# Output copy ahead of the gate's products, and the first two attentions laid out anew, in an attention and expert kernel

## The chip, the cores and the metric

The kernel runs on one core of one Trainium2 chip. The metric is the device time of one execution in microseconds (us). The engines are TensorE (PE), VectorE (DVE), ScalarE (ACT), GpSimd (POOL) and SyncE (SP). DMAs are issued from SP's, ScalarE's and GpSimd's queues.

## The reference

Attention over 8 batches with 16 query heads on 4 key heads, 384 positions and a head size of 64, and behind it a two-level gate that sends each position to one of 16 experts. An expert is two matrices with a relu between them.

```python
q (8, 16, 384, 64)   k, v (8, 4, 384, 64)
k, v = np.repeat(k, 4, axis=1), np.repeat(v, 4, axis=1)
attn = softmax(q @ k.transpose(0, 1, 3, 2) / 8)
x = (attn @ v).transpose(0, 2, 1, 3).reshape(3072, 1024)

g_idx = argmax(x @ w_group);  g_w = its softmax weight        # 4 groups
e_idx = argmax(x @ w_expert[g]);  e_w = its softmax weight    # 4 experts in each
h = np.maximum(x @ w1[g, e], 0.0)                             # 1024 x 1024
out = (g_w * e_w)[:, None] * (h @ w2[g, e])                   # 1024 x 1024
```

## The kernel before, in words

The work goes batch by batch, and every engine's order is written out by hand: the scheduler is off for the whole body. Behind the body a loop handles positions whose expert was not the one fetched for their batch; it runs no times here.

**One attention** (class `Attn`) has 24 units: four key heads, six blocks of 64 keys each. At step `u`, `run` scores unit `u + 2` on TensorE (`score`, which also issues the exponential on ScalarE into a tile `e`), multiplies unit `u` with the values (`pv`), and calls `tail`. At every second unit `tail` adds two exponential tiles on GpSimd (`pair`), unless the unit is in `apart`. `lags` tells at which step VectorE reduces which pair to row sums (`reduce`; a unit in `apart` gives two reductions in place of an addition and one). After six units the products are copied out of PSUM to `xT`, on ScalarE for the heads in `act_copies`, on VectorE for the others. The `steps` dictionaries add further work behind given steps.

**Sums and division.** `join_keys` adds the partial sums on VectorE, `sums` spreads them over the partitions by a small matmul and takes the reciprocal, `normalise(b, m)` makes a tile `rb` of the factors (a transpose) and multiplies `xT` by it, and `cast(b, m)` makes the bf16 copy `xb` that the expert's first matmuls (`moe_h`) read. There are four `m` to a batch.

**PSUM.** `ps_tile` deals out two buffers for scores and expert products ("s") and two for products, sums and gate ("o"); "x" takes the "o" buffer that is not the current one.

**A block.** While one batch's attention has ended, `block(b)` does the expert of batch `f = b - 1`: `moe_h`, then three chunks of `ffn_y`, with the sums, divisions and gate of batch `b` between them, and the first two scores of batch `b + 1`. `y_out(f, c, y)` is the output copy: ScalarE multiplies chunk `c` of the expert's products by the gate's weight on the way from PSUM to `ot`, and two DMAs on SP's queue write it out (with `late`, VectorE does it).

**Loads.** Weights (fetched as soon as the expert number is known, by `pick_w1` and `pick_w2`), keys and queries come by DMAs from GpSimd's queue with a cast to bf16; keys and queries are then transposed by DMAs on SP's queue (`before_attention`). The weights of batch `b` are used in the block after the one that fetches them. Values come by SP's queue, and `sum_v` adds them up on GpSimd for a guess of the expert.

Of the kernel before, what the change touches and what calls it, by code (L numbers as in the profile page):

```python
# [9 lines left out]
F32 = mybir.dt.float32  # L10
# [8 lines left out]
def kernel(  # L19
# [11 lines left out]
    nc = tc.nc  # L31
# [24 lines left out]
    qpool = ctx.enter_context(tc.tile_pool(name="qload", bufs=2))  # L56
    vpool = ctx.enter_context(tc.tile_pool(name="v", bufs=2))
    epool = ctx.enter_context(tc.tile_pool(name="exp", bufs=13))
# [41 lines left out]
    def load_q(b, src=None):  # L100
        qraw[b] = qpool.tile([P, KQ, NC * D], BF16, name="q_raw")
        nc.gpsimd.dma_start(out=qraw[b], in_=rows(q[b] if src is None else src))
# [311 lines left out]
    def normalise(b, m, which=None):  # L414
        if b not in xb:
            xb[b] = xpool.tile([P, KQ, S], BF16, name="xb")
        ks = slice(2 * m, 2 * m + 2)
        rb = ps_tile(which)[:, :, :S] if which else gpool.tile([P, 2, S], F32, name="rb")
        nc.vector.transpose(  # L419
            out=rb.rearrange("p k (j x) -> p k j x", x=32),  # L420
            in_=inv[b][:, ks].unsqueeze(3).to_broadcast([P, 2, NB, 32]))
        x = xT[b][:, ks, :]
        nc.vector.tensor_mul(out=x, in0=x, in1=rb)  # L423

    def cast(b, m):
        ks = slice(2 * m, 2 * m + 2)
        nc.scalar.copy(out=xb[b][:, ks, :], in_=xT[b][:, ks, :])  # L427
# [205 lines left out]
    def before_attention(b):  # L633

        if b + 1 < B:
# [8 lines left out]
    at = {0: Attn(0, apart=(1, 3, 7, 9, 17, 23), act_copies=(0, 1, 3), lags={3: [1, 3], 7: [5, 7], 9: [9], 12: [11], 16: [13], 18: [15], 21: [17], 23: [19]}),  # L644
          1: Attn(1, apart=(3, 5), act_copies=(3,), lags={5: [1], 8: [3], 10: [5], 12: [7, 9], 13: [11], 15: [13], 18: [15], 20: [17], 22: [19], 23: [21]})}
# [21 lines left out]
    def x_logits(b):  # L667
# [13 lines left out]
        17: [do(pick_w1, 0), do(join_keys, 0, 0, 2), do(pick_w2, 0)],  # L681
        22: [do(sums, 0, 0, 2, "x")],
        23: [do(at[0].reduce, NU - 3)],
# [8 lines left out]
    def first_softmax():  # L692
# [6 lines left out]

    steps1 = {  # L700
        1: [
            do(at[0].reduce, NU - 1),
            do(normalise, 0, 0),
            do(cast, 0, 0),
            do(normalise, 0, 1, "x"),
        ],
        3: [do(join_keys, 0, 2, Hkv), do(sums, 0, 2, Hkv, "x"), do(cast, 0, 1)],
        6: [do(normalise, 0, 2, "x"), do(normalise, 0, 3, "x")],
        8: [do(load_k, 2)],
        9: [do(cast, 0, 2), do(load_q, 2)],  # L710
        10: [do(cast, 0, 3)],
        14: [do(moe_h, 0, 0, "s"), x_gate_logits],
        15: [
# [9 lines left out]
        18: [do(join_keys, 1, 0, 2), do(before_attention, 1)],  # L723
# [5 lines left out]
    def first_block():  # L729
        load_v(3)  # L730
        moe_y(0, 0, "s")
        load_k(3)
        load_q(3)
        sum_v(2)
        at[1].reduce(NU - 1)
        join_keys(1, 2, Hkv)
        normalise(1, 1)
        cast(1, 0)
        cast(1, 1)
        moe_y(0, 1, "s")  # L740
        sums(1, 2, Hkv, "o")
        normalise(1, 2)
        normalise(1, 3)
        cast(1, 2)
        y = ffn_y(w2s[0], hTs[0], 2, "o", (0,))
        at[2] = Attn(2)
        at[2].score(0)
        ffn_y(w2s[0], hTs[0], 2, "o", (1,), y)
        at[2].score(1)
        return do(y_out, 0, 2, y, True)  # L750
# [16 lines left out]
    def block(b):  # L767
# [4 lines left out]
        if b + 2 < B:  # L772
            load_k(b + 2)
            load_q(b + 2)
        pick_w1(b)
        pick_w2(b)
        if not last:
            sum_v(b + 1)
        moe_h(f, 0, "s")
# [21 lines left out]
        cast(b, 3)  # L801
        gate_logits(b, pt)
# [4 lines left out]
        y_out(f, 1, y)  # L807
        if not last:
            at[b + 1].score(1)
# [148 lines left out]
```

## Time and profile before

| | |
|---|---|
| median of 3 runs | 395.7 us (395.08 to 395.71) |
| profiled execution | 394.66 us |
| its span in the profile | 393.0 us |
| busy: TensorE, VectorE, ScalarE, GpSimd | 93%, 65%, 58%, 52% |
| TensorE's mean granted clock | 0.973 of full speed |

The span runs from the first to the last instruction of the profiled execution; 1.66 us of its time lie outside. Busy shares are means over stages that have different limits. The granted clock is a share of TensorE's full 2.4 GHz; in any moment it is at 1.0 (2.4 GHz) or at 0.5 (1.2 GHz), and a figure between is a mean over a stretch.

### The profile page before, as it was taken

How to read it: one execution, taken by the hardware profiler on the slowest of the kernel's cores; microseconds unless marked ns; L12 is line 12 of the kernel's file. 1: busy time of each engine (PE TensorE's matmuls, PEld its weight loads, DVE VectorE, ACT ScalarE, POOL GpSimd, SP SyncE). 2: the span in 40 equal slices, each digit the busy share in tenths (PEclk: the TensorE clock that was granted, in tenths of full speed). 3: DMA queues.
4: the chain of work that ended last, by engine and by line, in shares of the span. 5: the costliest groups of instructions: out<-in, count | busy, mean ns of one | idle time of the engine just before them, and what ended most of it. 6: DMA issues, size and time to landing. Idle time of an engine off the chain costs nothing.

```text
span 393.0 us, 9216 instructions
## 1 busy us (share of the span) xinstructions
PE 365.5 (93%) x3815; PEld 186.7 (48%) x3815; DVE 255.4 (65%) x470; ACT 226.2 (58%) x298; POOL 203.5 (52%) x156
## 2 busy tenths in 40 slices
PE   7996999999999899989999899998999989999993
PEld 3442455445554345544555445543455445464541
DVE  3989775886787576844778446784567756684121
ACT  4895755478634496444944459343792539634330
POOL 8175481946980199503993059920698009930000
PEclk9999899999999899998999989998999999999997
DMA  8969995999989993999929999399993993079924
GB/s 198 192 108 207 213 194 80 185 253 211 180 157 203 251 212 105 131 236 235 201 56 167 229 233 185 66 177 224 215 177 51 211 237 96 3 126 201 261 55 111
DMA packets 69325, 67.14 MB, mean 171 GB/s; under 512 B 37112, under 2 KB 49400, under 8 KB 69280
## 3 DMA queue, kind: packets, MB, share of 16 engines
q0 software_dynamic: 26640, 41.03, 60.5%
q1 hardware_dynamic: 42288, 25.01, 29.4%
q8 instruction: 32, 0.52, 0.5%
q10 hardware_dynamic: 352, 0.48, 0.5%
q14 instruction: 13, 0.11, 0.1%
HBM read 86.07 MB, written 12.58 MB: 251 GB/s over the span
## 4 chain that ended last, share of the span: by engine, by line
PE 71%; DVE 15%; ACT 6%; issue 3%; POOL 3%; DMA 1%; SPq 0%; POOLq 0%; DVEq 0%; ACTq 0%
PE ps_o L327 27%; PE ps_s L588 11%; PE ps_s L602 10%; PE ps_o L602 8%; PE ps_s L308 8%; DVE xT L423 4%; DVE rb L419 4%; PE ps_o L435 3%; DVE inv L412 3%; POOL e L335 3%; DVE red L344 2%; ACT e L314 2%; ACT xb L427 2%; ACT ot L621 1%; PE ps_o L588 1%
## 5 line engine op out<-in xcount | busy, mean ns | idle before, releaser
L335 POOL TENSOR_TENSOR e<-e 128x768 f32<-128x768 f32 x88 | 157.3, 1823 | 128.3 <-PE ps_s L308 114.9
L314 ACT ACTIVATE e<-ps_s 128x768 f32<-128x768 f32 x192 | 151.7, 813 | 49.9 <-PE ps_s L308 47.8
L327 PE MATMUL ps_o<-e,v_raw 64*64 64x384 f32 x1536 | 155.0, 487 | 0.4 <-DVE oh_all L539 0.4
L344 DVE TRANSPOSE_TENSOR_REDUCE red<-e 128x24 f32<-128x768 f32 x104 | 99.6, 971 | 43.3 <-POOL e L335 42.8
L588 PE MATMUL ps_s<-xb,w 128*128 128x384 bf16 x480 | 80.8, 326 | 0.0
L308 PE MATMUL ps_s<-qT,kT 64*64 64x384 bf16 x768 | 65.6, 329 | 11.6 <-ACT ot L621 9.6
L327 PEld LDWEIGHTS ps_o<-e,v_raw 64*64 64x64 f32 x1536 | 56.2, 134 | 38.9 <-issue 30.4
L588 PEld LDWEIGHTS <-w 128*128 128x128 bf16 x512 | 49.4, 98 | 36.0 <-issue 4.8
L602 PEld LDWEIGHTS <-hT 128*128 128x128 bf16 x384 | 37.7, 102 | 54.5 <-issue 12.9
L602 PE MATMUL ps_s<-w,hT 128*128 128x512 bf16 x248 | 57.3, 379 | 2.2 <-ACT hT L595 1.4
L308 PEld LDWEIGHTS <-kT 64*64 64x64 bf16 x768 | 24.6, 106 | 48.9 <-issue 45.8
L592 ACT ACTIVATE hT<-ps_s 128x768 bf16<-128x768 f32 x23 | 18.6, 810 | 43.4 <-PE ps_s L588 39.1
L427 ACT CAST xb<-xT 128x768 bf16<-128x768 f32 x28 | 23.2, 830 | 29.1 <-DVE xT L423 29.1
L602 PE MATMUL ps_o<-w,hT 128*128 128x512 bf16 x136 | 37.9, 439 | 0.0
L419 DVE STREAM_TRANSPOSE rb<-inv 128x768 f32<-128x768 f32 x28 | 27.3, 977 | 0.9
L423 DVE TENSOR_TENSOR xT<-xT,rb 128x768 f32<-128x768 f32 x27 | 26.7, 989 | 1.0
L369 DVE COPY xT<-ps_o 128x768 f32<-128x768 f32 x27 | 24.9, 922 | 1.3 <-PE ps_o L327 1.3
L621 ACT ACTIVATE ot<-ps_s,we 128x1024 f32<-128x1024 f32 x14 | 15.6, 1114 | 10.0 <-PE ps_s L602 9.2
L456 DVE STREAM_TRANSPOSE gl<-ps_o 128x96 f32<-128x96 f32 x8 | 2.3, 283 | 23.1 <-PE ps_o L448 18.3
L618 DVE TENSOR_SCALAR ot<-ps_o,we 128x512 f32<-128x512 f32 x12 | 8.5, 747 | 12.9 <-PE ps_o L602 12.8
L412 DVE RECIPROCAL inv<-ps_o 64x96 f32<-64x96 f32 (+1 forms) x20 | 12.6, 631 | 6.2 <-PE ps_o L403 6.0
L507 POOL DMA_DIRECT2D w<-in_moe_w_dram x8 | 7.2, 905 | 12.3 <-DVE we L570 10.0
(123 smaller groups left out, 178.6 us busy)
## 6 DMA issues: line engine op xcount, KB each, us to landing
w<-in_moe_w_dram POOLq DMA_DIRECT2D x16, 2048.0 KB, 22.4
out_dram<-ot SPq DMA_DIRECT2D x42, 256.0 KB, 6.7
q_raw<-in_q_dram POOLq DMA_DIRECT2D x7, 768.0 KB, 9.2
v_raw<-in_v_dram SPq DMA_DIRECT2D x7, 384.0 KB, 4.5
out_dram<-ot SPq DMA_DIRECT2D x12, 128.0 KB, 2.4
k_raw<-in_k_dram POOLq DMA_DIRECT2D x7, 192.0 KB, 3.7
w<-in_q_dram POOLq DMA_DIRECT2D x3, 192.0 KB, 7.0
w<-in_q_dram ACTq DMA_DIRECT2D x2, 192.0 KB, 3.3
```

The costliest lines, as they stand in the source:

```text
L308: nc.tensor.matmul(out=sT[r * H2:(r + 1) * H2, s, :S], lhsT=kT[b][s * D:(s + 1) * D, key_block(b, s, g // 2, c), ks], rhs=qT[b][s * D:(s + ...
L314: nc.scalar.activation(e.rearrange("p t (s x) -> p s t x", s=2), sT[:, :, :S].rearrange("p s (t x) -> p s t x", t=2), ACT.Exp, scale=scale)
L327: nc.tensor.matmul(out=oT[t * D:(t + 1) * D, r, :S], lhsT=vraw[b][r * H2:(r + 1) * H2, g // 2, c * D:(c + 1) * D], rhs=self.e[u][r * H2:(r ...
L335: nc.gpsimd.tensor_add(out=self.e[u - 1], in0=self.e[u - 1], in1=self.e[u])
L344: nc.vector.tensor_reduce(out=red3[b][:, g, parts[b][g]].rearrange("p t j -> p (t j)"), in_=self.e[w].rearrange("p t (j x) -> p (t j) x", ...
L369: nc.vector.tensor_copy(out=dst, in_=src)
L412: nc.vector.reciprocal(out=iv[ts], in_=sm[ts, :, :, t])
L419: nc.vector.transpose(out=rb.rearrange("p k (j x) -> p k j x", x=32), in_=inv[b][:, ks].unsqueeze(3).to_broadcast([P, 2, NB, 32]))
L423: nc.vector.tensor_mul(out=x, in0=x, in1=rb)
L427: nc.scalar.copy(out=xb[b][:, ks, :], in_=xT[b][:, ks, :])
L588: nc.tensor.matmul(out=h[:, jj, :S], lhsT=w1[:, head_pair(m), (f0 + jj) * P:(f0 + jj + 1) * P], rhs=x[:, m, :], start=(m == 0), stop=(m == ...
L602: nc.tensor.matmul(out=y[:, nh, :], lhsT=hT[:, f, c * P:(c + 1) * P], rhs=w2[:, f, nh * HALF:(nh + 1) * HALF], start=(f == 0), stop=(f == ...
```

## The change

1. In `block`, the output copy of chunk 1, `y_out(f, 1, y)`, is issued before the gate's products and the first score of the next batch; before, it was issued between the first and the second score.
2. In `block`, the loads of keys and queries for batch `b + 2` are issued behind the weights and behind `sum_v`, no longer ahead of them. In `first_block` `sum_v(2)` goes ahead of the loads for batch 3.
3. The first two attentions get other tables: fewer units of the first batch are `apart`, other steps for the reductions, and for the first batch's sums, divisions and casts. The four casts of the first batch go from ScalarE to GpSimd.
4. The factors' tile of `normalise` comes out of the pool of exponential tiles, which has 16 buffers in place of 13; the four divisions of the first batch all use it. Before, three of these four had their factors in PSUM.
5. Queries have one load buffer in place of two.

```diff
-    qpool = ctx.enter_context(tc.tile_pool(name="qload", bufs=2))
-    epool = ctx.enter_context(tc.tile_pool(name="exp", bufs=13))
+    epool = ctx.enter_context(tc.tile_pool(name="exp", bufs=16))
...
-        qraw[b] = qpool.tile([P, KQ, NC * D], BF16, name="q_raw")
+        qraw[b] = lpool.tile([P, KQ, NC * D], BF16, name="q_raw")
...
-        rb = ps_tile(which)[:, :, :S] if which else gpool.tile([P, 2, S], F32, name="rb")
+        rb = ps_tile(which)[:, :, :S] if which else epool.tile([P, 2, S], F32, name="e")
...
-    def cast(b, m):
+    def cast(b, m, eng=None):
         ks = slice(2 * m, 2 * m + 2)
-        nc.scalar.copy(out=xb[b][:, ks, :], in_=xT[b][:, ks, :])
+        if eng is None:
+            nc.scalar.copy(out=xb[b][:, ks, :], in_=xT[b][:, ks, :])
+        else:
+            eng.tensor_copy(out=xb[b][:, ks, :], in_=xT[b][:, ks, :])
...
-    at = {0: Attn(0, apart=(1, 3, 7, 9, 17, 23), act_copies=(0, 1, 3), lags={3: [1, 3], 7: [5, 7], 9: [9], 12: [11], 16: [13], 18: [15], 21: [17], 23: [19]}),
-          1: Attn(1, apart=(3, 5), act_copies=(3,), lags={5: [1], 8: [3], 10: [5], 12: [7, 9], 13: [11], 15: [13], 18: [15], 20: [17], 22: [19], 23: [21]})}
+        0: Attn(0, apart=(1, 3, 23), act_copies=(0, 1, 3),
+                lags={3: [1], 4: [3], 8: [5], 10: [7], 12: [9], 14: [11], 17: [13], 19: [15],
+                      21: [17]}),
+        1: Attn(1, apart=(9, 11), act_copies=(3,),
+                lags={12: [1], 13: [3], 14: [5], 15: [7], 16: [9], 17: [11, 13], 19: [15],
+                      20: [17], 22: [19], 23: [21]}),
...
-        17: [do(pick_w1, 0), do(join_keys, 0, 0, 2), do(pick_w2, 0)],
-        22: [do(sums, 0, 0, 2, "x")],
-        23: [do(at[0].reduce, NU - 3)],
+        16: [do(join_keys, 0, 0, 2)],
+        17: [do(pick_w1, 0), do(pick_w2, 0)],
+        19: [do(sums, 0, 0, 2, "x")],
+        20: [do(normalise, 0, 0)],
...
-        1: [
-            do(at[0].reduce, NU - 1),
-            do(normalise, 0, 0),
-            do(cast, 0, 0),
-            do(normalise, 0, 1, "x"),
+        0: [do(at[0].reduce, NU - 1)],
+        1: [do(normalise, 0, 1)],
+        2: [do(at[0].reduce, NU - 5)],
+        4: [do(cast, 0, 0, pool), do(at[0].reduce, NU - 3), do(join_keys, 0, 2, Hkv)],
+        6: [do(cast, 0, 1, pool), do(load_k, 2), do(load_q, 2)],
+        10: [
+            do(sums, 0, 2, Hkv, "x"),
+            do(normalise, 0, 2),
+            do(normalise, 0, 3),
         ],
-        3: [do(join_keys, 0, 2, Hkv), do(sums, 0, 2, Hkv, "x"), do(cast, 0, 1)],
-        6: [do(normalise, 0, 2, "x"), do(normalise, 0, 3, "x")],
-        8: [do(load_k, 2)],
-        9: [do(cast, 0, 2), do(load_q, 2)],
-        10: [do(cast, 0, 3)],
-        14: [do(moe_h, 0, 0, "s"), x_gate_logits],
-        15: [
+        13: [do(cast, 0, 2, pool)],
+        15: [do(cast, 0, 3, pool)],
+        17: [
+            do(moe_h, 0, 0, "s"),
+            x_gate_logits,
             do(moe_h, 0, 2, "s"),
...
-        if b + 2 < B:
-            load_k(b + 2)
-            load_q(b + 2)
         pick_w1(b)
         pick_w2(b)
         if not last:
             sum_v(b + 1)
+        if b + 2 < B:
+            load_k(b + 2)
+            load_q(b + 2)
...
         cast(b, 3)
+        y_out(f, 1, y)
         gate_logits(b, pt)
         if not last:
             guess_logits(vm, guess_out(pt))
             at[b + 1] = Attn(b + 1)
             at[b + 1].score(0)
-        y_out(f, 1, y)
-        if not last:
             at[b + 1].score(1)
```

**ScalarE, end of the block of batch 3.** The rows before run from the relu of the expert's first products to the weights of the gate. `xb<-xT` is a cast, `ot<-ps_s,we` an output copy (chunk 0, then chunk 1), `e<-ps_s` an exponential (units 0 and 1 of the next batch).

```order
L595 ACTIVATE hT<-ps_s_2216 128x384 x2
L427 CAST xb<-xT 128x768
L621 ACTIVATE ot<-ps_s_2239,we 128x1024
L427 CAST xb<-xT 128x768
L314 ACTIVATE e<-ps_s_2316 128x2x2x192
L621 ACTIVATE ot<-ps_s_2261,we 128x1024
L314 ACTIVATE e<-ps_s_2327 128x2x2x192
L492 ACTIVATE ex<-sh 128x24
```

The same place in the changed kernel:

```order
L597 ACTIVATE hT<-ps_s_2215 128x384 x2
L427 CAST xb<-xT 128x768
L623 ACTIVATE ot<-ps_s_2238,we 128x1024
L427 CAST xb<-xT 128x768
L623 ACTIVATE ot<-ps_s_2260,we 128x1024
L313 ACTIVATE e<-ps_s_2319 128x2x2x192
L313 ACTIVATE e<-ps_s_2326 128x2x2x192
L494 ACTIVATE ex<-sh 128x24
```

The second output copy now stands ahead of both exponentials. The other four blocks that score a next batch read alike.

**GpSimd, from the first weights' fetch to the second batch's `sum_v`.** `e<-e` is an addition of a pair, `k_raw` and `q_raw` are the loads of batch 2. Before:

```order
L513 DMA w_490<-in_moe_w_dram 128x8x1024
L335 TENSOR_TENSOR e<-e 128x768 x4
L97 DMA k_raw<-in_k_dram 128x2x384
L335 TENSOR_TENSOR e<-e 128x768
L102 DMA q_raw<-in_q_dram 128x8x384
L335 TENSOR_TENSOR e<-e 128x768 x3
L113 TENSOR_TENSOR vs<-v_raw 128x384
```

In the changed kernel (`xb<-w_297` is a cast of the first batch, whose `xT` lies in a weight buffer):

```order
L515 DMA w_489<-in_moe_w_dram 128x8x1024
L334 TENSOR_TENSOR e<-e 128x768 x4
L429 CAST xb<-w_297 128x768
L334 TENSOR_TENSOR e<-e 128x768
L429 CAST xb<-w_297 128x768
L96 DMA k_raw<-in_k_dram 128x2x384
L101 DMA q_raw<-in_q_dram 128x8x384
L334 TENSOR_TENSOR e<-e 128x768 x2
L429 CAST xb<-w_297 128x768
L334 TENSOR_TENSOR e<-e 128x768
L429 CAST xb<-w_297 128x768
L334 TENSOR_TENSOR e<-e 128x768
```

Four casts came between the pairs; the last pair shown is followed by `sum_v` as before. Ahead of this place there are seven pairs where there were four.

**VectorE, the first batch's divisions.** `red<-e` is a reduction of exponentials, `inv<-ps_o` the reciprocal of the sums, `<-inv` the factors' transpose, and the line below it the multiplication of `xT`. Before:

```order
L412 RECIPROCAL inv<-ps_o_553 64x2x2x12 x2
L344 TENSOR_REDUCE red_267<-e 128x24 x4
L419 STREAM_TRANSPOSE rb<-inv 128x768
L423 TENSOR_TENSOR w_300<-w_300,rb 128x768
L419 STREAM_TRANSPOSE ps_o_606<-inv 128x2x384
L423 TENSOR_TENSOR w_300<-w_300,ps_o_606 128x768
L395 TENSOR_REDUCE red<-red_267 128x48
L412 RECIPROCAL inv<-ps_o_632 64x2x2x12 x2
```

In the changed kernel:

```order
L411 RECIPROCAL inv<-ps_o_516 64x2x2x12 x2
L418 STREAM_TRANSPOSE e<-inv 128x768
L422 TENSOR_TENSOR w_297<-w_297,e 128x768
L343 TENSOR_REDUCE red_264<-e 128x24 x3
L418 STREAM_TRANSPOSE e<-inv 128x768
L422 TENSOR_TENSOR w_297<-w_297,e 128x768
L343 TENSOR_REDUCE red_264<-e 128x24 x2
L394 TENSOR_REDUCE red<-red_264 128x24 x2
L368 COPY xT<-ps_o_582 128x768
L411 RECIPROCAL inv<-ps_o_718 64x2x2x12 x2
```

The first division is done ahead of three of the reductions, and the second sums' reciprocal (and so the sums' matmul on TensorE) stands behind the copy of the second batch's first head. The factors lie in a tile `e`, in SBUF, each time.

## Rows read from the trace of the kernel before

**Rows 1.** The page's first line.

```profile
span 393.0 us, 9216 instructions
```

**Rows 2.** Waits: engine, line, waited-for: us in total, times, longest.

```profile
PE ps_s L308 <- ACT ot L621: 9.6, 5, 1.9
```

**Rows 3.** Timeline near a block's end: start, us, engine, line, operation, [idle before].

```profile
172.81 1.53 PE L435 MATMUL ps_o<-xT,wg 128*32 128x96 f32 x64
...
174.41 0.36 PE L308 MATMUL ps_s<-qT,kT 64*64 64x384 bf16 x4
...
174.82 0.81 ACT L314 ACTIVATE e<-ps_s 128x768 f32<-128x768 f32 x1 [3.54 <-PE ps_s L308]
...
175.53 1.11 ACT L621 ACTIVATE ot<-ps_s,we 128x1024 f32<-128x1024 f32 x1
...
176.69 0.36 PE L308 MATMUL ps_s<-qT,kT 64*64 64x384 bf16 x4 [1.92 <-ACT ot L621]
...
177.86 0.15 DVE L555 CAST e_i<-ef 128x1 int32<-128x1 f32 x1
...
183.40 8.95 POOL L335 TENSOR_TENSOR e<-e 128x768 f32<-128x768 f32 x5 [20.63 <-PE ps_s L308]
```

**Rows 4.** Stretches of 5 us: busy of each engine, granted clock, DMA share, GB/s.

```profile
177.00:182.00 5.00, 5.00 (x20) 1.85 (x16) 2.02 (x12) 0.92 (x2) 0.00 (x0) 0.66 1.11 241
...
319.00:324.00 5.00, 5.00 (x44) 2.28 (x44) 3.35 (x14) 1.85 (x4) 0.22 (x1) 1.00 1.10 252
40.00:45.00 5.00, 5.00 (x48) 2.63 (x52) 3.02 (x5) 3.06 (x4) 0.00 (x0) 0.66 1.12 212
```

**Rows 5.** Timeline of TensorE in the first two attentions.

```profile
39.97 0.65 PE L403 MATMUL ps_o<-red,half 128*128 128x48 f32 x4 [4.50 <-DVE red L395]
...
45.49 0.33 PE L308 MATMUL ps_s<-qT,kT 64*64 64x384 bf16 x4
...
46.30 0.33 PE L308 MATMUL ps_s<-qT,kT 64*64 64x384 bf16 x4
...
50.46 0.36 PE L308 MATMUL ps_s<-qT,kT 64*64 64x384 bf16 x4 [0.48 <-ACT e L314]
...
52.20 2.77 PE L588 MATMUL ps_s<-xb,w 128*128 128x384 bf16 x16
```

**Rows 6.** Timeline of GpSimd, the first two attentions and one later.

```profile
6.42 0.82 POOL L133 CAST ot<-w 128x768 bf16<-128x768 f32 x1 [0.31 <-DMA w<-in_k_dram]
...
14.38 1.83 POOL L335 TENSOR_TENSOR e<-e 128x768 f32<-128x768 f32 x1 [4.66 <-PE ps_s L308]
...
27.64 0.92 POOL L507 DMA_DIRECT2D w<-in_moe_w_dram  x1 [2.26 <-DVE red L344]
...
135.96 21.40 POOL L335 TENSOR_TENSOR e<-e 128x768 f32<-128x768 f32 x12 [19.46 <-PE ps_s L308]
```

**Rows 7.** Timeline of VectorE and GpSimd around the values' sums.

```profile
56.66 0.46 POOL L114 TENSOR_TENSOR vs<-vs 128x128 f32<-128x128 f32 x1
...
79.01 1.00 DVE L423 TENSOR_TENSOR xT<-xT,rb 128x768 f32<-128x768 f32 x1
79.27 1.06 POOL L114 TENSOR_TENSOR vs<-vs 128x128 f32<-128x128 f32 x1
```

**Rows 8.** Timeline of VectorE in the second attention.

```profile
62.77 0.28 DVE L456 STREAM_TRANSPOSE gl<-ps_o 128x96 f32<-128x96 f32 x1 [2.48 <-PE ps_o L448]
...
67.41 0.95 DVE L369 COPY xT<-ps_o 128x768 f32<-128x768 f32 x1
68.27 0.97 DVE L344 TRANSPOSE_TENSOR_REDUCE red<-e 128x24 f32<-128x768 f32 x1
69.16 0.50 DVE L395 TENSOR_REDUCE red<-red 128x24 f32<-128x120 f32 x2
```

**Rows 9.** Tile of the weights, 157 to 161 us: the two issues' landing.

```profile
DMA to landing us min/median/max: 20.1/25.9/31.8
```

**Rows 10.** DMA issues, 150 to 200 us: count, us from issue to landing.

```profile
kT<-k_raw SPq DMA_TRANSPOSE x2, 13.6
qT<-q_raw SPq DMA_TRANSPOSE x1, 7.9
```

More of the change, by code (lines that the diff above doesn't have):

```diff
@@ L643 @@
     first_scores()
-    at = {0: Attn(0, apart=(1, 3, 7, 9, 17, 23), act_copies=(0, 1, 3), lags={3: [1, 3], 7: [5, 7], 9: [9], 12: [11], 16: [13], 18: [15], 21: [17], 23: [19]}),
-          1: Attn(1, apart=(3, 5), act_copies=(3,), lags={5: [1], 8: [3], 10: [5], 12: [7, 9], 13: [11], 15: [13], 18: [15], 20: [17], 22: [19], 23: [21]})}
+    at = {
+        0: Attn(0, apart=(1, 3, 23), act_copies=(0, 1, 3),
[4 more added lines that the diff above has]
+                      20: [17], 22: [19], 23: [21]}),
+    }
     at[0].start()
@@ L698, in first_softmax @@
         out_weights(0)
+    pool = nc.gpsimd
     steps1 = {
-        1: [
-            do(at[0].reduce, NU - 1),
-            do(normalise, 0, 0),
-            do(cast, 0, 0),
-            do(normalise, 0, 1, "x"),
-        ],
-        3: [do(join_keys, 0, 2, Hkv), do(sums, 0, 2, Hkv, "x"), do(cast, 0, 1)],
-        6: [do(normalise, 0, 2, "x"), do(normalise, 0, 3, "x")],
-        8: [do(load_k, 2)],
-        9: [do(cast, 0, 2), do(load_q, 2)],
-        10: [do(cast, 0, 3)],
-        14: [do(moe_h, 0, 0, "s"), x_gate_logits],
-        15: [
+        0: [do(at[0].reduce, NU - 1)],
[7 more added lines that the diff above has]
+            do(normalise, 0, 3),
+        ],
+        13: [do(cast, 0, 2, pool)],
[3 more added lines that the diff above has]
+            x_gate_logits,
             do(moe_h, 0, 2, "s"),
@@ L722 @@
         ],
-        18: [do(join_keys, 1, 0, 2), do(before_attention, 1)],
+        19: [do(before_attention, 1)],
+        20: [do(join_keys, 1, 0, 2)],
         21: [do(sums, 1, 0, 2, "x")],
@@ L731, in first_block @@
         moe_y(0, 0, "s")
+        sum_v(2)
         load_k(3)
         load_q(3)
-        sum_v(2)
         at[1].reduce(NU - 1)
```

## The prediction

> **What bounds the kernel now.** I read the page first: one core, a span of 393.0 us [rows 1]. TensorE is named at the head of the chain that ended last and is busy nearly everywhere, so the question is where it stands still and where it runs slowly. The view of waits for TensorE answers the first: five waits of the scores' matmuls for the output copy on ScalarE, 9.6 us in all, the longest 1.9 [rows 2]; the one other large wait is 4.50 us for a reduction on VectorE, once [rows 5].
>
> The timeline of one block (batch 3 is in its block here) shows where the five waits come from [rows 3]. After the gate's products (1.53 us from 172.81) TensorE scores unit 0 of the next batch at 174.41. ScalarE takes that unit's exponential at 174.82 and only then the output copy, at 175.53 for 1.11 us. The second score needs the PSUM buffer that the copy reads, and TensorE stands still for 1.92 us until 176.69.
>
> The view of stretches answers the second question. In the 5 us behind this wait the granted clock was 0.66 on the mean [rows 4]: part of the stretch at 2.4 GHz, part at 1.2 GHz. The same figure, 0.66, stands behind four of the five waits, and also behind the single wait of 4.50 us; behind the fifth wait it was 1.00 [rows 4]. A stretch of 5 us at 0.66 loses (1 - 0.66) x 5 = 1.7 us.
>
> **The change, part by part.** *The output copy ahead of the gate's products.* In the new order the copy follows the last cast, waits for the second half of its products, and runs while TensorE does the gate. Those products end where the gate's begin, at 172.81. The copy takes 1.11 us and TensorE does not come to the first score before 174.41, 1.6 us later, so 0.5 us are left over before the buffer is wanted [rows 3]. Its cover is the gate's 1.53 us; without it the whole 1.11 us would be seen. The first exponential waits for the first score in either order, so ScalarE loses nothing. The copy's two DMAs go out earlier on SP's queue and stand ahead of the next transposes as before. Gain: five waits, 9.6 us.
>
> With the wait gone I expect the slow stretch behind it to go: 4 x 1.7 = 6.8 us. Nothing in the rows names another cause for it, and all five slow stretches that I count in the middle of the program begin behind a still TensorE. The ends for this term are 0 and 6.8; I take 6.8.
>
> What is late next? TensorE would begin the next attention 1.92 + 1.7 us earlier. GpSimd's first pair starts at 183.40, with TensorE; before it GpSimd must load the expert number that VectorE writes at 177.86 to 178.01 [rows 3]. In the first attention the weights' fetch followed at 27.64 after 2.26 us of waiting for such a number [rows 6]. Even with 1.5 us for the load, 179.5, the first pair at 183.40 - 3.62 = 179.8 would not be held. So the gain is kept by what follows.
>
> *The first two attentions.* A unit there (scores and products) takes 46.30 - 45.49 = 0.81 us of TensorE [rows 5]. What TensorE loses there before the change: 4.50 us waiting for the second half of the first batch's key sums, 1.7 us of slow clock behind it [rows 4], and 0.48 us waiting for an exponential that stands behind a cast on ScalarE [rows 5]; 6.7 us. The change asks for those sums seven units later and takes the casts off ScalarE, so all three should go. Against that stand three new waits.
>
> First, GpSimd. From the first pair at 14.38 it hardly rests in the new order. Until the fourth cast it has 15 pairs (nine of the first batch, six of the second) at 8.95 / 5 = 1.79 us [rows 3], 26.9; two weight issues at 0.92 and two of keys and queries that I count alike, 3.6; the wait for the expert number, 2.26; and four casts [rows 6]. No row shows this cast; the nearest is a GpSimd cast of the same 128x768 fp32 elements to bf16, 0.82 us [rows 6]. A pair, 1.79 us, with two inputs, is the upper bound. I take 0.82, so 3.3. The sum puts the fourth cast's end at 14.38 + 26.9 + 3.6 + 2.26 + 3.3 = 50.4. TensorE comes to the first expert products at 52.20 before [rows 5]; in the new order three units stand ahead of them (2.4) and the 6.7 are gone: 47.9. The first batch's own first sums add to that: they now stand three units earlier, and their PSUM buffer is free only when VectorE has done a reduction and a copy, 0.97 and 0.95 [rows 8], which TensorE overtakes in part; between 0 and 1.9 I take 0.7, so 48.6. Six of the eight row blocks of the first products need only the first three casts, 6 / 16 of 2.77 = 1.0 us, so TensorE waits from 49.6 to 50.4: 0.8.
>
> Second, that 0.7 itself. Third, the second batch's first sums. VectorE's softmax chain takes from 62.77 to 67.41 = 4.64 us, then two reductions (1.8) and a join (0.5) stand ahead of them [rows 8]: 6.9 us. TensorE has one set of expert products (2.77 us, as at 52.20) and four units (3.2) in that time, 6.0. It waits 0.9. Together 0.7 + 0.8 + 0.9 = 2.4, and the gain would be 6.7 - 2.4 = 4.3.
>
> Here a row speaks against the change. At 79.01 VectorE multiplies two tiles that both lie in SBUF, and the small GpSimd sum that starts at 79.27 takes 1.06 us, where the same sum takes 0.46 at 56.66: it ends just behind the multiplication [rows 7]. The new kernel does four such multiplications among GpSimd's pairs, where three of the four read the factor from PSUM before. Each can push GpSimd back by its 1.0 us; three of them, at least, stand before the fourth cast. That is up to 3.0 us more waiting, and the gain 1.3.
>
> The Trainium skill, page "SBUF — State Buffer", section on practical consequences, says that a VectorE instruction with two SBUF inputs and a GpSimd instruction that reads SBUF exclude each other for the whole instruction. This trace agrees at 79.27 (1.06 us for 0.46). [...]
>
> I take the middle of 4.3 and 1.3, 2.8, less half a slow stretch (0.9), since a wait of two to three microseconds may bring one: 1.9. The ends: 6.7 if no new wait shows, and -2.7 if casts cost as much as pairs (four more microseconds) and the 1.3 is all that was left.
>
> *The rest.* Sixteen exponential buffers in place of 13 and the factor's tile among them: no row of before shows TensorE waiting long for an exponential buffer, so nothing, where GpSimd keeps up. Weights ahead of keys and queries in each block: nothing, since the weights are wanted a block later; see the last rival. One query buffer: its load now waits for the transposes of the batch before, which are issued a whole attention earlier.
>
> *The sum.* 9.6 + 6.8 + 1.9 = 18.3. The profiled execution took 394.66 us (span 393.0 and 1.66 around it) and would take 376.4. The median of the runs is 395.7, 1.0 above it; I move it by the same: 377.4.
>
> **The rivals.** *The clock falls anyway.* The slow stretches may belong to the place and not to the wait: TensorE passes there from small products to long ones. For it: the fifth wait had no slow stretch behind it, so a wait of 1.92 us is not enough by itself. Against: the same 0.66 stands behind the wait of 4.50 us, at quite another place and between other instructions. Then 6.8 stays, in whole or in part: up to 395.7 - 9.6 - 1.9 = 384.2.
>
> *GpSimd becomes the bound of the second attention.* The exponentials of its later units wait for buffers that late pairs hold, and the expert products for the casts. For it: 50.4 against 49.6 leaves nothing in hand. With casts at the price of pairs this part ends 2.7 below nothing: 395.7 - 16.4 + 2.7 = 382.0. The other way, all 6.7 gained: 372.6.
>
> *The wait is renamed.* If the copy were held by its cast or its weights, the second score would still wait: about 394. Against: the last cast is done before the products that the copy reads are.
>
> *Slower: the transposes come late.* Keys and queries now land behind the weights on GpSimd's queue, and SP stands at the key transposes until they do. The second of two weights lands 31.8 us after issue [rows 9], near 190 for an issue at 158; the keys some 4 us on (an estimate), 194; their transposes 13.6 us after issue, 207.6; the queries' 7.9 us after that, 215.5 [rows 10]. The value sums, too, now stand ahead of these loads on GpSimd, but the weights hide that. The scores want the transposes one batch after 174.41, at 174.41 + 47.4 - 3.6 = 218 (47.4 us is what a batch takes now, from the pairs' start at 135.96 to that at 183.40 [rows 3, 6]). It decides from 2.5 us of further delay; each microsecond beyond that counts in four blocks. To end slower, more than 18.3 us must be lost, 4.6 in each of four: from 7 us of delay on. At 10 us the time would be about 377.4 + 4 x 7.5 = 407.
>
> **How the numbers follow.** My forecast, waits and slow stretches gone and -0.5 to 4.5 us from the first two attentions: 374.8 to 379.8, chance 0.48. More than that from them: 371 to 374.8, 0.12. The clock falls anyway: 380 to 386, 0.18. GpSimd the bound: 380 to 386, 0.12. The wait renamed: about 394 to 396, 0.05. Late transposes: 397 or more, 0.05. The range 371 to 386 holds the first four, 0.90 with their spread a little less. A measurement of this kernel tells 0.2%, 0.8 us, from no change. Faster 0.92, same 0.03, slower 0.05.
>
> **What would show it.** Right: no wait of the scores for the output copy; granted clock 1.00 in the 5 us behind the two scores; the output copy during the gate's products; no wait of 4.50 us near 35 to 40; GpSimd without rest from 14 to 50 and its fourth cast near 50 to 54, with TensorE waiting there for it by 1 to 4 us. Wrong: 0.66 behind the scores with no wait ahead of it; TensorE waiting for transposed queries or keys at a block's end; GpSimd's cast at 1.8 us; exponentials in the second attention waiting for pairs.

## The result

The changed kernel takes 377.28 us (median of 4 runs, 377.12 to 377.49), the kernel before 395.62 us in the same comparison: the ratio is 0.954, with an interval of 0.9523 to 0.9556. The forecast was 377.4. That the total came so near is luck: its terms are off in opposite directions, and the errors cancel. Two kernels below had one execution each that was far longer (1301 and 534 us); their medians, 373.56 and 377.49 us, are told without it (373.92 and 377.67 with it).

The page of the changed kernel, its first line (the profiled execution took 377.12 us):

```profile
span 375.3 us, 9195 instructions
```

TensorE's largest wait after the change (engine, line, waited-for: us in total, times, longest):

```profile
PE ps_o L402 <- DVE xT L368: 3.0, 1, 3.0
```

The line of [rows 2] is gone: no score waits for the output copy. This wait of 3.0 us, which [rows 5] did not have, now stands at the head. It lies in the first two attentions.

The block of [rows 3] after the change (timeline: start, us, engine, line, operation, [idle before]):

```profile
169.74 1.53 PE L437 MATMUL ps_o<-xT,wg 128*32 128x96 f32 x64
169.84 1.12 ACT L623 ACTIVATE ot<-ps_s,we 128x1024 f32<-128x1024 f32 x1 [1.64 <-PE ps_s L604]
...
171.34 0.52 PE L307 MATMUL ps_s<-qT,kT 64*64 64x384 bf16 x8
```

The copy runs under the gate's products and ends at 170.96, 0.4 us before the scores; both scores follow each other without a stop. The view of stretches (busy of each engine, granted clock, DMA share, GB/s), answering to [rows 4]:

```profile
46.00:51.00 5.00, 4.86 (x44) 2.48 (x48) 4.00 (x7) 2.24 (x3) 2.23 (x2) 0.66 1.11 211
171.00:176.00 5.00, 4.84 (x52) 2.23 (x46) 3.90 (x23) 1.92 (x4) 0.00 (x0) 1.00 1.04 253
```

Behind the scores the clock is 1.00 in all five blocks (one is shown). The one stretch at 0.66 follows the new wait of 3.0 us.

**Where the time went, by a landmark.** The guess of the next batch's expert is a pair of small matmuls on TensorE at each block's end. It started at 126.88, 174.27, 221.72, 269.17 and 316.34 before, and at 127.95, 171.20, 214.44, 257.69 and 300.94 after. A batch went from 47.4 to 43.25 us, 4.1 us less, four times. Up to the first landmark the change lost 1.1 us: the second expert products of the first batch begin at 73.69, where before they began at 72.50.

That loss is in the first two attentions. The first multiplication of the first batch and the second expert products before (timeline of the kernel before):

```profile
36.67 0.96 DVE L423 TENSOR_TENSOR w<-w,rb 128x768 f32<-128x768 f32 x1
...
72.50 7.08 PE L602 MATMUL ps_s<-w,hT 128*128 128x512 bf16 x32
```

The timeline of the changed kernel there:

```profile
30.56 7.16 POOL L334 TENSOR_TENSOR e<-e 128x768 f32<-128x768 f32 x4
31.06 7.48 DVE L422 TENSOR_TENSOR w<-w,e 128x768 f32<-128x768 f32 x1
38.60 0.82 POOL L429 CAST xb<-w 128x768 bf16<-128x768 f32 x1 [0.89 <-DVE w L422]
...
39.49 0.36 PE L307 MATMUL ps_s<-qT,kT 64*64 64x384 bf16 x4 [1.15 <-ACT e L313]
...
43.06 0.82 POOL L429 CAST xb<-w 128x768 bf16<-128x768 f32 x1 [1.84 <-DVE w L422]
...
45.13 0.96 DVE L368 COPY xT<-ps_o 128x768 f32<-128x768 f32 x1
46.14 0.65 PE L402 MATMUL ps_o<-red,half 128*128 128x48 f32 x4 [3.04 <-DVE xT L368]
...
46.90 1.45 PE L326 MATMUL ps_o<-e,v_raw 64*64 64x384 f32 x8
...
50.17 1.82 POOL L334 TENSOR_TENSOR e<-e 128x768 f32<-128x768 f32 x1 [2.77 <-PE ps_o L326]
...
50.82 1.99 DVE L422 TENSOR_TENSOR w<-w,e 128x768 f32<-128x768 f32 x1
51.93 1.56 POOL L429 CAST xb<-w 128x768 bf16<-128x768 f32 x1
...
55.22 0.81 POOL L429 CAST xb<-w 128x768 bf16<-128x768 f32 x1
...
56.09 1.79 PE L590 MATMUL ps_s<-xb,w 128*128 128x384 bf16 x10 [0.75 <-POOL xb L429]
...
73.69 7.08 PE L604 MATMUL ps_s<-w,hT 128*128 128x512 bf16 x31
```

VectorE's first multiplication took 7.48 us instead of 0.96. GpSimd's four pairs beside it took 7.16 us, 1.79 each, just as without it: GpSimd was not held. VectorE was, to the end of the fourth pair; before, no pair ran beside its 0.96 us. All that VectorE does behind it is late: ScalarE's next exponential waits for it (and TensorE 1.15 us for that), the copy of the second batch's first head comes at 45.13, and the second sums wait 3.04 us for it.

### The profile page after: what moved, and what is told of

The parts are those of the page before. It is cut to its first block, busy times and chain, and to the rows that moved or that the text cites. A ratio compares the mean times of both kernels' runs of the same rounds, so it can differ in the third digit from the quotient of the medians.

```text
span 375.3 us, 9195 instructions
## 1 busy us (share of the span) xinstructions
PE 356.2 (95%) x3800; PEld 184.3 (49%) x3815; DVE 257.4 (69%) x469; ACT 224.1 (60%) x294; POOL 211.3 (56%) x163
## 4 chain that ended last, share of the span: by engine, by line
PE 72%; DVE 19%; ACT 3%; issue 2%; POOL 2%; DMA 1%; SPq 0%; POOLq 0%; DVEq 0%
PE ps_o L326 27%; PE ps_s L604 12%; PE ps_s L590 10%; PE ps_s L307 8%; PE ps_o L604 6%; DVE e L418 4%; DVE xT L422 3%; PE ps_o L437 3%; DVE inv L411 3%; DVE red L343 3%; DVE w L422 2%; ACT xb L427 2%; PE ps_o L590 1%; PE ps_o L402 1%; ACT e L313 1%
## 5 line engine op out<-in xcount | busy, mean ns | idle before, releaser
L334 POOL TENSOR_TENSOR e<-e 128x768 f32<-128x768 f32 x91 | 162.7, 1822 | 101.5 <-PE ps_s L307 87.5
L343 DVE TRANSPOSE_TENSOR_REDUCE red<-e 128x24 f32<-128x768 f32 x101 | 96.7, 971 | 38.5 <-POOL e L334 38.4
L307 PE MATMUL ps_s<-qT,kT 64*64 64x384 bf16 x768 | 64.4, 328 | 2.9 <-ACT e L313 2.3
L604 PEld LDWEIGHTS <-hT 128*128 128x128 bf16 x384 | 36.0, 98 | 48.5 <-ACT hT L597 5.3
L604 PE MATMUL ps_o<-w,hT 128*128 128x512 bf16 x129 | 29.8, 379 | 1.0 <-issue 0.9
L418 DVE STREAM_TRANSPOSE e<-inv 128x768 f32<-128x768 f32 x31 | 30.1, 972 | 0.4
L422 DVE TENSOR_TENSOR xT<-xT,e 128x768 f32<-128x768 f32 x27 | 25.9, 958 | 1.0
L623 ACT ACTIVATE ot<-ps_s,we 128x1024 f32<-128x1024 f32 x14 | 15.6, 1114 | 17.2 <-PE ps_s L604 16.4
L422 DVE TENSOR_TENSOR w<-w,e 128x768 f32<-128x768 f32 x4 | 11.4, 2846 | 0.2
```

The source lines that it names most:

```text
L307: nc.tensor.matmul(out=sT[r * H2:(r + 1) * H2, s, :S], lhsT=kT[b][s * D:(s + 1) * D, key_block(b, s, g // 2, c), ks], rhs=qT[b][s * D:(s + ...
L334: nc.gpsimd.tensor_add(out=self.e[u - 1], in0=self.e[u - 1], in1=self.e[u])
L343: nc.vector.tensor_reduce(out=red3[b][:, g, parts[b][g]].rearrange("p t j -> p (t j)"), in_=self.e[w].rearrange("p t (j x) -> p (t j) x", ...
L418: nc.vector.transpose(out=rb.rearrange("p k (j x) -> p k j x", x=32), in_=inv[b][:, ks].unsqueeze(3).to_broadcast([P, 2, NB, 32]))
L604: nc.tensor.matmul(out=y[:, nh, :], lhsT=hT[:, f, c * P:(c + 1) * P], rhs=w2[:, f, nh * HALF:(nh + 1) * HALF], start=(f == 0), stop=(f == ...
```

## The experiments

The theory after the result: (a) the output copy's waits and the slow stretches behind them are worth about 17 us; (b) a multiplication with both inputs in SBUF is shut out while GpSimd adds pair after pair, and this ate the gain of the first two attentions; (c) some 0.35 us per block come from the factor's tile and the order of the loads. The rivals stand with each run. Line numbers of a kernel built on the one before are by one or two other than those of one built on the changed one.

**The copy alone.** The kernel before, with only the copy moved.

```diff
         cast(b, 3)
+        y_out(f, 1, y)
         gate_logits(b, pt)
...
             at[b + 1].score(0)
-        y_out(f, 1, y)
-        if not last:
             at[b + 1].score(1)
```

> The kernel before with one edit: the output copy of chunk 1 ahead of the gate's products. From one batch to the next the changed kernel gained 4.1 us where a slow stretch went with the wait and 2.2 where there was none. Theory: of these the copy gives 2.1 (the wait) and 1.7 (the clock), and 0.3 to 0.4 per block come from something else in the change. Then 5 x 2.1 + 4 x 1.7 = 17.3, and this kernel takes 395.6 - 17.3 = 378.3. Rival: all that the blocks gained is the copy's, 18.7, and this kernel takes 376.9. Second rival: the clock falls without the wait, and it takes 385. By either of the first two the layout of the first two attentions is worth nothing or a loss of about 1 us.

Measured: 378.38 us, ratio 0.9576 (0.9527 to 0.9624), 17.3 us less than before. Three of the four batches take 43.6 us, the fourth 43.37, and the clock is 1.00 behind all five scores. This one move is nearly the whole effect. What the block still lacks against 43.25 shows in its timeline around the first division:

```profile
159.31 0.45 POOL L115 TENSOR_TENSOR vsum<-vs 128x128 bf16<-128x128 f32 x1
159.35 1.23 DVE L423 TENSOR_TENSOR xT<-xT,rb 128x768 f32<-128x768 f32 x1
...
162.20 1.46 PE L602 MATMUL ps_s<-w,hT 128*128 128x512 bf16 x6 [0.26 <-ACT hT L592]
...
163.90 1.42 PE L602 MATMUL ps_s<-w,hT 128*128 128x512 bf16 x5 [0.23 <-ACT hT L595]
```

The last value sum stretches the multiplication from 0.96 to 1.23; the next transpose waits for the one factor tile; ScalarE's casts and relus come later, and TensorE waits twice. In the fourth batch the value sum is over before the multiplication begins.

**The copy put back.** The changed kernel, with the copy between the two scores again (the reverse of that diff).

> The changed kernel with the output copy back between the two scores. Theory: five waits of about 1.9 us return, and with most of them the slow stretch behind it, granted clock near 0.66 over 5 us: 377.3 + 17.3 = 394.6, less 1.7 for each wait without a slow stretch. Rival: the wait costs its own 10.6 alone and the clock stays, 387.9.

Measured: 393.44 us (10 runs, 391.11 to 394.93), ratio 0.9955 (0.9923 to 0.9988). All five waits are back, of 1.98 us each, but in the profiled execution only two of the five have a slow stretch behind them. The 16 expert products behind the second score, in the batch-3 block and in the next one (timeline of TensorE):

```profile
175.54 0.36 PE L307 MATMUL ps_s<-qT,kT 64*64 64x384 bf16 x4 [1.98 <-ACT ot L623]
175.83 3.63 PE L604 MATMUL ps_o<-w,hT 128*128 128x512 bf16 x16
...
220.96 0.36 PE L307 MATMUL ps_s<-qT,kT 64*64 64x384 bf16 x4 [1.98 <-ACT ot L623]
221.25 5.31 PE L604 MATMUL ps_o<-w,hT 128*128 128x512 bf16 x16
```

The same instructions behind the same wait took 3.63 us once and 5.31 us the other time. A batch takes 45.4 us without a slow stretch and 47.1 with one. So a wait costs 45.42 - 43.25 = 2.17 us and a slow stretch 1.68 us, each measured by itself. The rival, 387.9 with the clock at full speed, lies below all ten runs. The single runs lie near 391.2, 393 and 394.7, as two, three and four slow stretches would give. Their mean clocks agree for the first two groups (0.982, then 0.977 to 0.979), but three of the four longest runs have 0.979 too and only the one of 394.93 us has 0.970, so what made those three longer is open.

**Half of the copy put back.** The first 512 columns ahead of the gate, the others between the scores (`y_half` copies one half on ScalarE into the same tile, and issues the two DMAs behind the second).

```diff
         cast(b, 3)
-        y_out(f, 1, y)
+        ot = y_half(f, 1, y, 0)
         gate_logits(b, pt)
...
             at[b + 1].score(0)
+        y_half(f, 1, y, 1, ot)
+        if not last:
             at[b + 1].score(1)
```

> The changed kernel with half of the output copy (512 of 1024 columns) put back between the two scores; the other half stays ahead of the gate. A copy of 128x512 took 0.69 us where the whole one takes 1.11, so TensorE's wait is 1.98 - 0.42 = 1.56 us, five times. A block without a slow stretch then takes 43.25 + 2.17 - 0.42 = 45.0 us, with one 46.7. Theory: a wait of this kind is often followed by a slow stretch, also where it is somewhat shorter: 1 to 4 of 5 blocks take 46.7, and the median is 377.3 + 5 x 1.75 + 1.7 to 6.8 = 387.7 to 392.8. Rival: the clock falls only behind waits as long as the 1.92 and 1.98 us seen so far: no block of 46.7, and the median is 386.0.

Measured: 386.04 us, ratio 0.977 (0.9729 to 0.9812). My theory fell and the rival's 386.0 was met. The view of waits and the stretch behind one of them:

```profile
PE ps_s L307 <- ACT ot L630: 7.8, 5, 1.6
```

```profile
176.00:181.00 5.00, 5.00 (x50) 2.31 (x51) 3.01 (x12) 2.07 (x5) 1.05 (x1) 1.00 1.11 265
```

Five waits of 1.56 us, no slow stretch behind any, and a batch of 45.0 us: 1.75 us a wait.

**The first two factors in PSUM.** The changed kernel; two of the first batch's four divisions take their factors from PSUM.

```diff
-        20: [do(normalise, 0, 0)],
+        20: [do(normalise, 0, 0, "x")],
...
-        1: [do(normalise, 0, 1)],
+        1: [do(normalise, 0, 1, "x")],
```

> The changed kernel with the factors of the first batch's first two divisions in PSUM, as the kernel before has them for the second. In the changed kernel the first of these multiplications, with both inputs in SBUF, took 7.48 us and ended just behind a run of four GpSimd pairs. Theory: VectorE is shut out as long as GpSimd reads SBUF without a gap. With the factors in PSUM the multiplication takes about 0.96 us, the wait of 3.04 us for the second half of the sums and the slow stretch behind it (1.7) go, and the wait of 1.15 us for an exponential; GpSimd's fourth cast, near 52, then holds TensorE for 2 to 3 us. 377.3 - 5.9 + 1 to 3 = 372.5 to 374.5. Rival: the multiplication waits for something else (a buffer, a semaphore) and takes as long; no change, 377.3.

Measured: 373.56 us, ratio 0.9454 (0.9413 to 0.9495): 3.7 us better than the changed kernel. Its timeline:

```profile
30.74 7.18 POOL L334 TENSOR_TENSOR e<-e 128x768 f32<-128x768 f32 x4
31.25 0.95 DVE L422 TENSOR_TENSOR w<-w,ps_o 128x768 f32<-128x768 f32 x1
...
41.68 0.65 PE L402 MATMUL ps_o<-red,half 128*128 128x48 f32 x4
...
42.83 3.60 POOL L334 TENSOR_TENSOR e<-e 128x768 f32<-128x768 f32 x2
...
44.33 2.93 DVE L422 TENSOR_TENSOR w<-w,e 128x768 f32<-128x768 f32 x1
...
51.67 3.35 PE L590 MATMUL ps_s<-xb,w 128*128 128x384 bf16 x10 [2.22 <-POOL xb L429]
```

Beside the same four pairs the multiplication takes 0.95 us when one input lies in PSUM, and the second sums (41.68) no longer wait. The third multiplication, still with both inputs in SBUF, meets two pairs and takes 2.93 us. This is (b). What remains is a wait of 2.22 us for the fourth cast.

**The second sums earlier.** On top of that kernel.

```diff
-        10: [
+        8: [
             do(sums, 0, 2, Hkv, "x"),
             do(normalise, 0, 2),
             do(normalise, 0, 3),
         ],
-        13: [do(cast, 0, 2, pool)],
-        15: [do(cast, 0, 3, pool)],
+        12: [do(cast, 0, 2, pool), do(cast, 0, 3, pool)],
```

> The kernel with the first two factors in PSUM (373.92 us), and the second key sums of the first batch asked for at unit 8 of the second attention in place of 10, with the third and fourth casts on GpSimd ahead of the pair of unit 13. Theory: what is left of the loss there is TensorE's wait of 2.22 us for the fourth cast (51.67) and 1.7 us of slow clock behind it, and the cast is late only because the multiplications ahead of it are asked for late and are shut out behind pairs (2.93 and 2.54 us for 0.96). Then the fourth cast ends before 49.4, the wait and the slow stretch are gone, and the median is 373.9 - 3.9 = 370.0, between 369.5 and 371.5. Rival: the multiplications collide with the same pairs one by one earlier, or the pairs that now stand behind the casts hold back the reductions and so the second batch's sums by as much: 373 to 374.5.

Measured: 370.76 us, ratio 0.9388 (0.9348 to 0.9427), the best of all kernels here. Its timeline:

```profile
42.02 0.96 DVE L422 TENSOR_TENSOR w<-w,e 128x768 f32<-128x768 f32 x1
42.12 2.53 POOL L334 TENSOR_TENSOR e<-e 128x768 f32<-128x768 f32 x1
43.91 1.57 DVE L422 TENSOR_TENSOR w<-w,e 128x768 f32<-128x768 f32 x1
44.62 2.30 POOL L429 CAST xb<-w 128x768 bf16<-128x768 f32 x2
...
47.34 2.77 PE L590 MATMUL ps_s<-xb,w 128*128 128x384 bf16 x16
```

The third multiplication begins 0.1 us ahead of the pair, and now GpSimd is the one that is held (2.53 for 1.8 us). The casts end at 46.92, and all 16 first expert products run in one piece.

**Two factor tiles.** The copy-alone kernel, with two buffers for the factor and one for queries.

```diff
-    qpool = ctx.enter_context(tc.tile_pool(name="qload", bufs=2))
+    qpool = ctx.enter_context(tc.tile_pool(name="qload", bufs=1))
...
-        rb = ps_tile(which)[:, :, :S] if which else gpool.tile([P, 2, S], F32, name="rb")
+        rb = ps_tile(which)[:, :, :S] if which else gpool.tile([P, 2, S], F32, name="rb", bufs=2)
```

> The kernel of the run with the copy alone, with two factor tiles in place of one (and one query buffer, which makes room). Theory: in each of six blocks the four transposes and multiplications no longer wait for one another's tile, 1.88 us a division in place of 2.01, so casts and relus on ScalarE come earlier and TensorE's two waits of about 0.25 us for relus go: 6 x 0.35 = 2.1 less than the copy alone, 376.2. Rival: the block gained from the order of the loads (the value sums no longer run beside the first multiplication), and this kernel takes what the copy alone takes.

Measured: 377.49 us, ratio 0.9553 (0.9512 to 0.9594), and a batch of 43.50 us: 0.14 of the 0.39 us. This is neither the theory's 376.2 nor the rival's unchanged 378.4. TensorE's second wait is gone, but the first multiplication still takes 1.22 us beside the last value sum, and the first wait stays (timeline):

```profile
159.04 1.22 DVE L423 TENSOR_TENSOR xT<-xT,rb 128x768 f32<-128x768 f32 x1
...
161.89 3.41 PE L602 MATMUL ps_s<-w,hT 128*128 128x512 bf16 x13 [0.26 <-ACT hT L592]
```

**The loads first again.** The changed kernel with keys and queries ahead of weights and value sums in `block`.

```diff
+        if b + 2 < B:
+            load_k(b + 2)
+            load_q(b + 2)
         pick_w1(b)
         pick_w2(b)
         if not last:
             sum_v(b + 1)
-        if b + 2 < B:
-            load_k(b + 2)
-            load_q(b + 2)
```

> The changed kernel with one part undone: in each block, keys and queries are loaded ahead of the weights and of the value sums again, as before the change. Theory: the 0.26 us per block that the copy and the factor's tile do not explain (a block takes 43.64 us with the copy alone, 43.50 with two factor tiles as well, 43.25 in the changed kernel) comes from this order, because the value sums on GpSimd then start 1.2 us earlier and are over before VectorE's first multiplication of the block. Then a block takes 43.50 us here, the first multiplication 1.22 us in place of 0.96, TensorE waits about 0.26 us for the expert's activations again, and the median is 4 to 5 times 0.25 above 377.3: 378.3 to 378.5. Rival: the order is worth nothing and the 0.26 us comes from the one query buffer or the sixteen exponential buffers: a block takes 43.25 us and the median is 377.3.

Measured: 377.87 us, ratio 0.9566 (0.9526 to 0.9606), 0.6 above the changed kernel and short of the 1.0 to 1.2 expected. Batches take 43.49, 43.29, 43.54 and 43.24 us. Two blocks of its timeline show why:

```profile
159.51 0.46 POOL L114 TENSOR_TENSOR vsum<-vs 128x128 bf16<-128x128 f32 x1
159.56 1.21 DVE L422 TENSOR_TENSOR xT<-xT,e 128x768 f32<-128x768 f32 x1
...
162.40 5.79 PE L604 MATMUL ps_s<-w,hT 128*128 128x512 bf16 x24 [0.24 <-ACT hT L594]
...
203.10 0.96 DVE L422 TENSOR_TENSOR xT<-xT,e 128x768 f32<-128x768 f32 x1
203.20 1.18 POOL L114 TENSOR_TENSOR vsum<-vs 128x128 bf16<-128x128 f32 x1
```

Whoever starts first runs through; the other waits. At 159.51 the value sum is first by 0.05 us and TensorE pays 0.24; at 203.10 the multiplication is first, the sum takes 1.18 us, and nobody waits for it. So the order costs a quarter of a microsecond in the blocks where the sum wins, two of four here. In the changed kernel the sums end 1.2 us before the first multiplication, at 158.51, and never meet it.

This trace shows one more thing. Behind the wait for the second sums, as long here as in the changed kernel, the clock did not fall: it is 1.00 in every stretch of 1 or 2 us from 46 to 58 (timeline of TensorE):

```profile
46.52 0.65 PE L402 MATMUL ps_o<-red,half 128*128 128x48 f32 x4 [3.03 <-DVE xT L368]
...
47.28 0.82 PE L326 MATMUL ps_o<-e,v_raw 64*64 64x384 f32 x8
...
55.97 1.78 PE L590 MATMUL ps_s<-xb,w 128*128 128x384 bf16 x10 [1.71 <-POOL xb L429]
```

The first products behind the wait took 0.82 us here and 1.45 in the changed kernel (46.90). Yet the second expert products began at 73.59, only 0.1 us earlier than in the changed kernel (0.5 if counted from the first guess of an expert, 24.32 here and 23.93 there): TensorE waited 1.71 us for the fourth cast in place of 0.75. At this place the slow stretch costs little, because GpSimd's cast sets the time behind it.

**Gaps between the pairs.** Three kernels tried to let the shut-out multiplication in: a short GpSimd instruction behind four of the pairs that sets one column to zero, one that copies one column to another (`tensor_copy` in place of `memset`, on a tile of two columns), and one that sets 160 columns to zero.

```diff
                 nc.gpsimd.tensor_add(out=self.e[u - 1], in0=self.e[u - 1], in1=self.e[u])
+                if (self.b, u) in ((0, 19), (0, 21), (1, 1), (1, 3)):
+                    nc.gpsimd.memset(gap, 0.0)
...
+    gap = cpool.tile([P, 1], F32, name="gap")
```

> The changed kernel with one instruction more behind four of GpSimd's pairs (units 19 and 21 of the first attention, 1 and 3 of the second): it sets a column of 128 numbers to zero, so it only writes. Theory: VectorE's multiplication of two SBUF tiles cannot get in while GpSimd's pairs, which read SBUF, follow each other without a gap, and any instruction between them that reads nothing lets it in. Then the multiplication that took 7.48 us from 31.06 takes at most 2.8 us (the rest of the pair under way, 1.8, and its own 0.96), TensorE's wait of 3.04 us for the second key sums of the first batch is gone, with the slow stretch of 1.7 us behind it, and the median is near that of the kernel with the factor in PSUM, 373.5 to 375. Rival: the multiplication is let in only where GpSimd really stands still (it waits for another engine); a short instruction in between is no such gap. Then it takes 7 us or more again and the median is 377.3 to 377.8.

> As the kernel with four short instructions that only write, but each of them copies one column of a small SBUF tile to another (one input, as a cast has, not two as a pair has). In the kernels run so far VectorE's multiplication got in between a pair and a cast each time (the changed kernel at 50.82, the kernel with early sums at 43.91), and never between a pair and a pair, nor where a column was set to zero between them (7.59 us). Theory: what lets it in is a GpSimd instruction with one SBUF input behind a pair. Then the multiplication takes at most 2.8 us, TensorE's wait of 3.04 us is gone, and the median is 373.5 to 375. Rival: it is the length of that instruction that counts (a cast takes 0.82 us, this copy about 0.1), or the cast's place; the multiplication takes 7 us or more and the time is 377.3 to 378.2.

> As the kernel with four short instructions that only write, but each sets 160 columns to zero in place of one, so that the stretch in which GpSimd reads nothing is longer. Theory of the length: a longer stretch lets VectorE's multiplication in at the first of them; it takes at most 3 us, the wait of 3.04 us is gone, and the time is 373.5 to 375. Rival: an instruction that only writes does not let it in, however long; the multiplication takes 7.6 us or more (four pairs and four of these), and the time is 377.5 to 379.

Measured: 378.02 us (ratio 0.9574, 0.9533 to 0.9616), 377.71 (0.9544, 0.9516 to 0.9572) and 377.65 (0.9543, 0.9515 to 0.957). None let it in; the multiplication took 7.59, 7.85 and 8.01 us. The rivals held all three times, though the first time lies 0.2 us above its rival's range. The timeline of the first:

```profile
30.67 7.59 DVE L424 TENSOR_TENSOR w<-w,e 128x768 f32<-128x768 f32 x1
31.95 0.11 POOL L336 MEMSET gap<- 128x1 f32 x1
32.00 1.82 POOL L334 TENSOR_TENSOR e<-e 128x768 f32<-128x768 f32 x1
```

and of the second, where the column is copied:

```profile
36.15 0.18 POOL L336 COPY gap<-gap 128x1 f32<-128x1 f32 x1
...
38.04 0.92 POOL L336 COPY gap<-gap 128x1 f32<-128x1 f32 x1
```

Only at the last of the copies, with no pair behind it, does the multiplication get in, and the copy waits (0.92 for 0.18 us).

## Why the prediction was right, and where it was not

*The output copy.* Right in its mechanism and a little too small. Predicted: 9.6 + 6.8 = 16.4; the copy alone brought 17.3. The wait's row shows the idle time only, 1.92 us; the two scores, too, run in 0.52 us together where each took 0.36 alone, 0.2 more. The copy-back kernel has 2.17 us for a wait of 1.98. Five times about 2.1 and four times 1.68 are 17.2.

*The clock.* The rival that it falls anyway is refuted: in the copy-alone kernel the same products follow the same scores with no stretch below 1.00 in any block. The argument against this rival was only in part good, though: a wait of 1.9 to 2.0 us brings a slow stretch in some executions and blocks and none in others, so the fifth wait of [rows 4] was not a different case. A wait goes ahead of every slow stretch seen, but not every wait brings one, not even the 3.03 us in the loads-first kernel.

*The first two attentions: this term failed.* Predicted +1.9; measured against the profile of before, the landmark moved from 72.50 to 73.69, -1.2. Against the copy-alone kernel, whose first two attentions are those of before but whose slow stretch there cost twice as much, it moved from 73.24, -0.45. The beginnings of the traces differ by as much (the first guess of an expert stands at 24.03 in the one and 23.62 in the other, whose code is the same up to there), so the -0.45 cannot be told from nothing. The step at fault is the weighing of the four multiplications, "Each can push GpSimd back by its 1.0 us". The exclusion was seen, but with the sides reversed: it was VectorE that stood back, for a run of four pairs and not for one instruction. Of the four multiplications two started during a pair and waited for it (31.06 and 50.82), and two met no pair and took 0.96 us (42.04 and 48.87). The old losses did go (4.50, 0.48 and 1.7). In their place came waits of 3.04, 1.15, 0.75, 0.49 and 0.78, 6.2 us, and a slow stretch of 1.7: 7.9 for 6.7, which is the 1.2. (The parts of this tally depend on one another: in the loads-first kernel, without the slow stretch, the wait for the fourth cast was 1.71 in place of 0.75.) The cast cost 0.82 as taken. That TensorE waited 0.75 us for the fourth cast and 0.78 for the second batch's first sums, where 0.8 and 0.9 were forecast, is luck, as TensorE was late itself: the cast ended at 56.03 and not at 50.4. Nor did GpSimd work without rest up to there: it stood for 0.89, 1.84 and 2.77 us, twice for VectorE's products and once for TensorE (38.60, 43.06, 50.17). With two factors in PSUM the change is worth 72.50 - 70.85 = 1.65 here, near the 1.9.

The Trainium skill, page "SBUF — State Buffer", section "SBUF: two separate sides", says that whichever of the two starts first gets the shared ports for the whole instruction. At single meetings these runs agree (159.51 and 203.10 in the loads-first kernel). So does the row that the prediction took its price from, where the multiplication started first (79.01 against 79.27 in [rows 7]); where it starts during a pair, by the same rule, it is VectorE that waits. For such a run the rule is too kind, and the measurement decides: VectorE did not get its turn when the first pair ended. That an operand in PSUM frees the multiplication (0.95 us beside four pairs) agrees with its condition of two SBUF inputs.

*"The rest": not nothing.* The factor's second buffer (tried together with one query buffer) is worth 0.14 us a block and the value sums ahead of the loads about 0.25 where they would have met the first multiplication, 1.6 us in all behind the first landmark (249.0 us from there to the end in the copy-alone kernel, 247.4 in the changed one). [rows 7] showed such a meeting, but it was priced in the first two attentions only. The sum that was measured: 17.3 + 1.6 = 18.9 against 18.3 in all. This leaves -0.6 for the first two attentions, between the two readings above.

*Late transposes.* The weights did go ahead, and keys and queries land 24.7 and 27.9 us after issue. But their transposes then took 5.1 and 5.6 us instead of the 13.6 and 7.9 of [rows 10], and nothing waited.

## What to carry to other kernels

Where a profile shows an engine standing still, ask what the clock does just behind it: a wait of two microseconds can cost nearly twice its length (2.17 and 1.68 us here). It need not, and a slow stretch costs little where the next wait takes it up. Before putting a VectorE instruction with two SBUF inputs beside GpSimd's steady work, find out who is in possession: a run of GpSimd additions kept it out for the whole run, while with one input in PSUM, or with a start just ahead of the addition, it lost nothing (in the second case GpSimd lost 0.7 us). When a total agrees with its forecast, check the terms against landmarks anyway; here 1.6 us that nobody had priced and 0.9 that were priced too low hid a shortfall of 2.5 (-0.6 in place of 1.9).

## What the runs showed that was not expected

A VectorE multiplication of 0.96 us stood 6.5 us behind four GpSimd additions in a row, without slowing them (1.79 us each), and short instructions between them did not let it in: to write 1 or 160 columns, or to copy one. Between a pair and a cast it did get in (2.30 us for two casts of 0.82 in the early-sums kernel). What decides this is open; neither one input nor a gap of 0.24 us is enough. The casts differ from the short instructions in one more way: they read what VectorE's multiplications wrote, so they have to wait for VectorE. Whether that lets the multiplication in was not tested.

Between 1.56 us of standing still (never a slow stretch, five waits) and 2.22 us (a slow stretch in the kernel with two factors in PSUM) lie 1.92 and 1.98 us, which had one in four of five and in two of five waits. Length alone does not decide: of the seven kernels profiled with a wait of 3.03 or 3.04 us for the second sums, six had a slow stretch behind it and the loads-first kernel had none. In the kernel with two factors in PSUM, too, three executions took 373.3 to 373.6 us at a mean clock of 0.996, and two, the profiled one among them, 374.3 to 374.6 us at 0.990 and 0.992. What decides between the two outcomes of one and the same wait is open. Nor is the price fixed: from 39 to 46 us, behind the wait of 4.5 us, the copy-alone kernel had a mean clock of 0.53 and the kernel before 0.76, so 3.3 us were lost for 1.7.
